# Requests to ScalarE that may pass one another, memsets and three products moved to VectorE, a DMA moved to GpSimd's queue, and another order on SyncE

## The chip, the cores and the metric

The kernel runs on one core of a Trainium2 chip. The core has five engines that work side by side, each through its own list of instructions in order: TensorE (PE, matrix products; PEld is its weight load), VectorE (DVE), ScalarE (ACT), GpSimd (POOL) and SyncE (SP), which here only issues DMAs. Semaphores order the lists against each other. The metric is the device time of one execution in microseconds; three executions of the kernel before took 570.37, 576.92 and 570.92 us, and their median, 570.92 us, is the time before.

## The reference

Two layers in a row. The first is a gated linear attention over 4 batches, 8 heads, 768 steps and 40 channels; the second a mixture of experts over the 3072 resulting rows of 320, each of which goes to the best two of eight experts by noisy gate values.

```python
for t in range(S):                       # per batch and head
    m_new = np.maximum(f_gate[:, :, t] + m, i_gate[:, :, t])
    f_stab = np.exp(f_gate[:, :, t] + m - m_new)
    i_stab = np.exp(i_gate[:, :, t] - m_new)
    m = m_new
    C = f_stab * C + i_stab * outer(vt, kt)
    n = f_stab * n + i_stab * kt
    y[:, :, t] = sigmoid(o_gate[:, :, t]) * (C @ qt) / maximum(abs(n @ qt), 1)

x = y.transpose(0, 2, 1, 3).reshape(3072, 320)
noisy = x @ w_gate + log1p(exp(x @ w_noise)) * noise
top2 = the best two columns of noisy;  w = exp(v - v.max()), divided by its sum + 1e-9
out[row] += w[k] * (relu(x[row] @ w1[e]) @ w2[e])      # for the two experts e of a row
```

All values are float32. The kernel keeps the matrix products of the experts near float32 precision by splitting each operand into a rounded high part and a low rest and adding three products.

## The kernel before

**Two stages.** The attention stage works in 24 units (`NU`), each of 64 steps of two groups of heads, so 128 rows of x. The expert stage takes the eight experts one after another: rows are gathered by token number, transposed, multiplied by w1 (L887), by w2 (L905 to L907), scaled, and added to the output by a scattered DMA (L931). All lists are written by hand in the order in which the program text runs; nothing reorders them later.

**A pass of the loop (L758).** Pass i works on several units at once, in this order of program text. The names are those of the prediction.

- At its head the DMAs: weights of choices that wait in the list `sent` (L762), the loads of unit i+3 (`load_unit`, L144 for q and k, L147 and L148 for v, k and the output gate), the copy of the rows of unit i-1 to DRAM (`keep_rows`, L377; POOL's queue issues it for units up to 11, SP's later), the moves of the gate values (`gate_move`, L212 and L214; POOL's queue up to pass 12, then SP's), pieces of w1 and w2 of the first expert (L117, L120, L724). Only four buffers exist for a unit's loads, so the v load of unit i+3 waits until unit i-1 is done with its buffer, and `keep_rows(i-1)` waits for the rows of i-1. SP takes these in order.
- `p_part(i+1)` (L337 on DVE): score products times decay weights, p(i+1).
- `c_part(i)` (L351 on PE, L354 on ACT): the state for the next unit. `o_part(i)` (L360 on PE): the output products, into PSUM bank o, of which there is one buffer. `e_part` (L298 on PE, L301 on ACT): decay exponents for unit i+2, one half here, one half later in the pass.
- `f_part(i)`, f(i) in the prediction (L365 to L373 on DVE): the division; then xr(i) (L374 on POOL): the product with the sigmoid of the output gate, 128 rows of x.
- logits of unit i-2 (`l_part`, L405 on PE), ranks that a group has asked for (`r_part`, L414 to L416), a burst that adds a group's token numbers to a table (`b_part`, L425, when no ranks are due), the transposes of rows i-1 (`t_part`, L385), and ACT's copies of all these (L389, L454, L457, L434).
- scores of unit i+2 (`s_part`, L319 and L323 on PE), the sigmoid of unit i+1 (`sig_part`, L306 to L308 on ACT), the decayed keys of unit i+2 (`k_part`, L331 on DVE).

**The routing (`g_part`, L470).** Four units make a group. When a group's logits are there, a generator puts its small operations into the lists bit by bit: `fill` (L629) lets it run at fixed places of a pass until a budget of estimated DVE time is used (1.8 us a pass), and a generator that yields "wait" gives up its turn. Its stages: softplus of the noise scale (exponent and logarithm on ACT), the best two by MAX8 and FIND_INDEX8 (L511, L514), d, the difference of the two (L517 on POOL), its exponent on ACT, the marks m and their running sums (L527, L535), ranks from PE (L559), places in the table (L575 to L589), weights (L549, L550), and the one-hot operands OA and OB of the burst (L596, L602). When four groups are in the table, `decode` (L438, on DVE) turns it into token numbers for the first four tiles of expert 0, and POOL issues their four gathers (L716) at the head of the last pass.

**ACT's requests.** The generator does not issue its ACT operations itself. It appends them to `acts`, and `act()` (L645), which stands at three places of a pass, issues all that are there. The generator waits until the list is empty, whoever filled it:

```python
acts.append((d, d, AF.Exp))          # L518, right behind d = P.tensor_sub(...)
...
while acts:                          # L537, ahead of the request for ranks
    yield "wait"
```

**The weights' way to DRAM.** A row of DRAM tile `rows` holds 320 values of x and then two weights. The generator computes the weights (L549, L550) as soon as d's exponent is there and appends the DMA to `sent`; SP issues it at the head of the next pass (L762), or in `tell` behind the loop.

**Constants.** `constants()` (L263) runs once, at pass 6: zeros in the unused half of w1's low part (64x1024), a row of zeros that later clears the output (128x320), the table (128x56) and the weights' tile (128x384), all by POOL, and a cast of token numbers by DVE (L265). Two more casts by DVE follow it (L793, L794).

## Time and profile before

| | us |
|---|---|
| median of three executions | 570.92 |
| the profiled execution | 572.61 |
| its span on the core | 570.5 |
| PE busy in the span | 545.3 |
| DVE busy | 352.4 |
| ACT busy | 254.9 |
| POOL busy | 244.0 |
| attention stage, until the first product of expert 0 | 151.7 |

The profiled execution's own time is 2.1 us above its span. How its rows are read: a row of a timeline starts with its start and its duration in us, then engine, source line, operation, output<-inputs by the program's names, shape and count; a bracket at its end tells how long the engine was idle before it and what ended that. A row of the windows view gives, for a stretch of time, each engine's busy time and its number of instructions, the clock granted to TensorE (1.00 is full) and the share of the DMA engines. A row of groups ends with busy time, mean ns of one, and the idle time before the group with its releasers. Busy time of PE is modelled from pipelined products, so a busy PE need not be at its peak.

### The profile page before, as it was taken

Reading aid. Unit: us, or ns where it says so; the run is one execution under the profiler, and the core shown is the slowest. Engines: PE = TensorE matmul, PEld = TensorE weight load, DVE = VectorE, ACT = ScalarE, POOL = GpSimd, SP = SyncE. Lnnn points to the kernel's source line nnn. Section 1 sums busy time; section 2 is a strip of 40 time slices with the busy share of each in tenths; the row PEclk is TensorE's granted clock in tenths of the full one; section 3 lists DMA queues with packets and bytes.
Section 4 is the critical chain, followed back from the end, with each engine's and each line's share of the span. In section 5 each row is a group of like instructions: output and inputs, shape, how many; then the busy total and the mean of one; then the engine's idle time right before and its main releaser. Section 6 shows DMA issues by size and latency. Waiting matters only on the chain.

```text
span 570.5 us, 13345 instructions
## 1 busy us (share of the span) xinstructions
PE 545.3 (96%) x5158; PEld 494.8 (87%) x5158; DVE 352.4 (62%) x937; ACT 254.9 (45%) x621; POOL 244.0 (43%) x336
## 2 busy tenths in 40 slices
PE   8799898999699999999999999999999999999995
PEld 3588787888479898998899899889989998998995
DVE  8889999998594386654563565466356545644511
ACT  6576778876241354522541442254145225414500
POOL 7446676533456546046224604532460453241043
PEclk9799899998699899999999999999999999999998
DMA  5887889795379365264326326432642543232023
GB/s 142 190 212 209 210 203 219 213 236 152 105 235 312 85 114 128 93 152 71 114 42 146 90 93 149 63 99 59 150 96 93 143 58 85 79 40 25 2 31 47
DMA packets 41060, 71.11 MB, mean 125 GB/s; under 512 B 8761, under 2 KB 30478, under 8 KB 40992
## 3 DMA queue, kind: packets, MB, share of 16 engines
q1 hardware_dynamic: 29632, 51.23, 31.8%
q0 software_dynamic: 11360, 18.98, 19.3%
q8 instruction: 42, 0.69, 0.5%
q14 instruction: 26, 0.21, 0.1%
HBM read 52.76 MB, written 17.73 MB: 124 GB/s over the span
## 4 chain that ended last, share of the span: by engine, by line
PE 80%; DVE 8%; DMA 5%; ACT 3%; issue 2%; POOL 1%; SPq 1%; POOLq 0%; DVEq 0%
PE s L887 22%; PE e L887 11%; PE st L907 5%; PE st L906 5%; PE st L905 5%; PE o L907 4%; PE o L906 4%; PE o L905 4%; PE s L746 3%; PE s L323 3%; DMA vk<-vk_in 2%; PE o L360 2%; PE e L298 2%; PE st L351 2%; PE xt L405 1%
## 5 line engine op out<-in xcount | busy, mean ns | idle before, releaser
L931 POOL DMA_INDIRECT y_out<-y,tok x56 | 87.1, 1556 | 220.5 <-DVE y L921 219.8
L887 PE MATMUL s<-xh,w1h 128*128 128x512 f32 (+1 forms) x255 | 78.0, 361 | 1.5 <-DVE xh L750 0.9
L893 DVE SCALAR_TENSOR_TENSOR hlo<-s,hh 128x512 fp32r<-128x512 f32 (+1 forms) x85 | 47.4, 558 | 41.2 <-ACT hh L892 36.7
L748 ACT ACTIVATE xh<-s 128x384 fp32r<-128x384 f32 (+1 forms) x56 | 25.4, 469 | 103.2 <-PE s L746 102.9
L716 POOL DMA_INDIRECT xg<-rows,tok x56 | 58.4, 1043 | 26.2 <-issue 16.8
L892 ACT ACTIVATE hh<-s 128x512 fp32r<-128x512 f32 (+1 forms) x85 | 41.7, 491 | 48.6 <-PE s L887 46.5
L887 PE MATMUL s<-xh,w1l 128*128 128x512 f32 (+1 forms) x255 | 63.1, 356 | 0.0
L905 PE MATMUL st<-w2h,hh 128*128 128x320 f32 x184 | 58.0, 315 | 0.0
L907 PE MATMUL st<-w2h,hlo 128*128 128x320 f32 x184 | 57.2, 311 | 0.0
L906 PE MATMUL st<-w2l,hh 128*128 128x320 f32 x184 | 56.8, 309 | 0.0
L887 PEld LDWEIGHTS s<-xh,w1h 128*128 128x128 f32 x255 | 46.2, 190 | 7.9 <-ACT xh L748 2.0
L905 PE MATMUL o<-w2h,hh 128*128 128x320 f32 x168 | 53.0, 315 | 0.0
L907 PE MATMUL o<-w2h,hlo 128*128 128x320 f32 x168 | 52.4, 312 | 0.0
L906 PE MATMUL o<-w2l,hh 128*128 128x320 f32 x168 | 51.9, 309 | 0.0
L887 PEld LDWEIGHTS s<-xh,w1l 128*128 128x128 f32 x255 | 45.1, 190 | 6.0
L887 PE MATMUL s<-xl,w1h 128*128 128x512 f32 (+1 forms) x170 | 46.6, 355 | 0.5 <-DVE xl L749 0.5
L374 POOL TENSOR_TENSOR xr<-tm,vk 128x320 f32<-128x320 f32 x24 | 22.2, 926 | 43.0 <-DVE tm L373 12.9
L887 PE MATMUL e<-xh,w1h 128*128 128x320 f32 (+1 forms) x129 | 39.7, 363 | 0.0
L749 DVE TENSOR_TENSOR xl<-s,xh 128x256 fp32r<-128x256 f32 (+1 forms) x56 | 22.6, 404 | 26.9 <-ACT xh L748 23.3
L323 PE MATMUL s<-qk 64*64 64x64 f32 x768 | 36.2, 233 | 0.7 <-issue 0.7
L921 DVE TENSOR_SCALAR y<-st,gw 128x320 f32<-128x320 f32 x23 | 12.7, 551 | 39.2 <-PE st L907 39.2
L893 DVE SCALAR_TENSOR_TENSOR hlo<-e,hh 128x256 fp32r<-128x256 f32 (+1 forms) x43 | 23.8, 554 | 18.8 <-ACT hh L892 17.9
(203 smaller groups left out, 1368.7 us busy)
## 6 DMA issues: line engine op xcount, KB each, us to landing
vk<-vk_in SPq DMA_DIRECT2D x48, 242.0 KB
raw<-w_in SPq DMA_DIRECT2D x7, 1280.0 KB
qk<-qk_in SPq DMA_DIRECT2D x48, 160.0 KB
raw<-w_in SPq DMA_DIRECT2D x7, 1024.0 KB
y_out<-zrow SPq DMA_DIRECT2D x15, 320.0 KB
raw<-w_in SPq DMA_DIRECT2D x18, 256.0 KB
rows<-xr POOLq DMA_DIRECT2D x12, 160.0 KB
rows<-xr SPq DMA_DIRECT2D x12, 160.0 KB
```

Of the source, the lines that this page charges most:

```text
L323: T.matmul(SQ[u][:, p][half[p], h, :], q[r, 1, h, :], q[r, 0, h, :], start=True, stop=True)
L374: P.tensor_mul(XR[u], tm.rearrange("p h d -> p (h d)"), SG[u % 4])
L716: P.indirect_dma_start(out=XG[0:rows_of(t), t], out_offset=None, in_=XD[0:n], in_offset=bass.IndirectOffsetOnAxis(ap=token(e, t), axis=0), ...
L748: A.activation(XH[:, :, c], ps[:, :, 0:n], AF.Copy)
L749: V.tensor_sub(XL[:, :, c], ps[:, 0:2, 0:n], XH[:, 0:2, c].bitcast(F32))
L887: T.matmul(ps[:, 0:n], l, r, start=i == 0, stop=i == len(ops) - 1)
L892: A.activation(HH[:, f, c], ps[:, 0:m], AF.Relu)
L893: V.scalar_tensor_tensor(HLO[:, f, c], ps[:, 0:m], 0.0, HH[:, f, c].bitcast(F32), op0=OP.max, op1=OP.subtract)
L905: T.matmul(ps, HH[:, j, c], W2H[:, j], start=j == 0, stop=False)
L906: T.matmul(ps, HH[:, j, c], W2L[:, j], start=False, stop=False)
L907: T.matmul(ps, HLO[:, j, c], W2H[:, j], start=False, stop=j == 7)
L931: st = P.indirect_dma_start(out=out, out_offset=bass.IndirectOffsetOnAxis(ap=token(e, t), axis=0), in_=y[0:n], in_offset=None, compute_op= ...
```

## The change

Five edits, all in the attention stage and in the routing.

1. `act()` keeps a count with each request, and `ask` makes one. A request with `late` 2 is issued at the third `act()` instead of the next; requests behind it are not held. Each generator waits for its own request alone. Only the exponent of d is asked for with `late` 2. The request for ranks now comes ahead of the wait for it.
2. The four memsets of `constants()` go to DVE, and the whole function, with the three casts, runs at pass 5.
3. The weights are computed at the end of the group's small operations, ahead of OA and OB, and POOL's queue issues their DMA there. `sent` stays empty.
4. At the head of a pass SP issues the q and k load, the gates' moves and the pieces of w1 and w2 first, and then the v load and the copy of rows, which wait for the unit before.
5. xr of units 21, 22 and 23 is computed by DVE instead of POOL.

```diff
+XP = 21
...
     def constants():
-        P.memset(W1L[0:64, 2].bitcast(F32), 0.0)
+        V.memset(W1L[0:64, 2].bitcast(F32), 0.0)
         V.tensor_copy(toki, cs[:, C_TOK:C_TOK + NU])
-        P.memset(zrow, 0.0)
-        P.memset(TBL, 0.0)
-        P.memset(WTS, 0.0)
+        V.memset(zrow, 0.0)
+        V.memset(TBL, 0.0)
+        V.memset(WTS, 0.0)
...
-        P.tensor_mul(XR[u], tm.rearrange("p h d -> p (h d)"), SG[u % 4])
+        (P if u < XP else V).tensor_mul(XR[u], tm.rearrange("p h d -> p (h d)"), SG[u % 4])
...
-        acts.append((ue, na, AF.Exp))
-        while acts:
+        a = ask(ue, na, AF.Exp)
+        while a[0] >= 0:
             yield "wait"
...
-        acts.append((d, d, AF.Exp))
+
+        a = ask(d, d, AF.Exp, 2)
...
         acc[g] = base[:, :, nb]
-        while acts:
+        rk = sm("rk", [128, NE * nb + 8])
+        asked = [m[:, :, 1:], base[:, :, 0:nb], base[:, :, nb], rk, False, unit[0] + (g < 3)]
+        want.append(asked)
+        while not asked[4] or a[0] >= 0:
             yield "wait"
         dd = sm("dd", [128, nb])
         P.tensor_scalar(dd, d, 1.0, 1e-9, op0=OP.add, op1=OP.add)
         e12 = OVM[:, u0:u0 + nb, 0:2]
         P.tensor_copy(e12, mi[:, :, 0:2])
-        yield
-        rk = sm("rk", [128, NE * nb + 8])
-        asked = [m[:, :, 1:], base[:, :, 0:nb], base[:, :, nb], rk, False, unit[0] + (g < 3)]
-        want.append(asked)
-        wt = WTS[:, u0:u0 + nb, 0:2]
-        yield "wait"
-        V.reciprocal(wt[:, :, 0], dd)
-        P.tensor_mul(wt[:, :, 1], d, wt[:, :, 0])
-        yield
-        sent.append((XD.rearrange("(u p) c -> p u c", p=128)[:, u0:u0 + nb, DM:RW], WTS[:, u0:u0 + nb]))
-        while not asked[4]:
-            yield "wait"
...
-        P.tensor_mul(OVM[:, u0:u0 + nb, 2:4], wt, ov)
         yield
         bi = sm("bi", [128, 2 * nb])
         V.scalar_tensor_tensor(bi, ai, -128.0, f(r), op0=OP.mult, op1=OP.add)
+        wt = WTS[:, u0:u0 + nb, 0:2]
+        yield
+        V.reciprocal(wt[:, :, 0], dd)
+        P.tensor_mul(wt[:, :, 1], d, wt[:, :, 0])
+        P.tensor_mul(OVM[:, u0:u0 + nb, 2:4], wt, ov)
+        P.dma_start(XD.rearrange("(u p) c -> p u c", p=128)[:, u0:u0 + nb, DM:RW], WTS[:, u0:u0 + nb])
...
     def act():
 
-        while acts:
-            A.activation(*acts.pop(0))
+        for a in list(acts):
+            if a[0] == 0:
+                A.activation(*a[1])
+                acts.remove(a)
+            a[0] -= 1
+
+    def ask(o, i, f, late=0):
+
+        a = [late, (o, i, f)]
+        acts.append(a)
+        return a
...
-        while sent:
-            SP.dma_start(*sent.pop())
         if 1 <= i and i + 3 < NU:
-            load_unit(i + 3)
-        if i:
-            keep_rows(i - 1)
+            load_unit(i + 3, "k")
...
             early_w2(2 * (i - W2AT), 2)
+
+        if 1 <= i and i + 3 < NU:
+            load_unit(i + 3, "v")
+        if i:
+            keep_rows(i - 1)
...
-        if i == 6:
+        if i == 5:
             constants()
```

More of the change, by code (lines that the diff above doesn't have):

```diff
@@ L488, in g_part @@
         ln = sm("ln", [128, nb, NE])
-        acts.append((ln, t1, AF.Ln))
+        a = ask(ln, t1, AF.Ln)
         co = sm("co", [128, nb, NE])
@@ L495, in g_part @@
         V.tensor_mul(co, co, na)
-        while acts:
+        while a[0] >= 0:
             yield "wait"
@@ L645, in act @@
     def act():
-        while acts:
-            A.activation(*acts.pop(0))
+        for a in list(acts):
[7 more added lines that the diff above has]
+        return a
     def warm(n):
```

## The prediction

> **What bounds the kernel now.** I read the page's head, slices and chain first, then busy time by stage, then the idle brackets of each engine's timeline in the attention stage.
>
> ```profile
> span 570.5 us, 13345 instructions
> ...
> PE 545.3 (96%) x5158; PEld 494.8 (87%) x5158; DVE 352.4 (62%) x937; ACT 254.9 (45%) x621; POOL 244.0 (43%) x336
> ...
> DVE  8889999998594386654563565466356545644511
> ```
>
> ```profile
> core 0: us, PE busy (x) PEld busy (x) DVE busy (x) ACT busy (x) POOL busy (x), PEclk, DMA share, GB/s
> ...
> 87.00:108.00 21.00, 20.31 (x456) 17.74 (x456) 20.12 (x64) 17.07 (x44) 10.75 (x20) 1.00 0.90 226
> ...
> 152.00:205.00 53.00, 51.20 (x291) 46.33 (x291) 30.27 (x106) 18.05 (x50) 28.41 (x42) 0.92 0.65 182
> ```
>
> The expert stage, from 152 us on, keeps PE busy (51.20 of 53.00) and the change leaves its matmuls alone. What can move is the attention stage before it, and there the averages mislead: DVE is at 62% over the span but at eight or nine tenths in the first ten slices. From 87 to 108 us PE and DVE are both full (20.31 and 20.12 of 21.00). Which of them bounds? PE has real holes there, and most end with ACT's exponent (the view of waits, 18 to 156 us: waiter, releaser, us, times, longest):
>
> ```profile
> PE e L298 <- ACT w L301: 5.5, 4, 2.4
> ...
> PEld s L319 <- DMA qk<-qk_in: 0.5, 2, 0.2
> ```
>
> DVE's timeline from 41 to 142 us carries an idle bracket on three rows alone:
>
> ```profile
> 67.15 0.69 DVE L559 TENSOR_TENSOR oh<-oh,rk 128x64 f32<-128x64 f32 x1 [0.77 <-ACT rk L457]
> ...
> 108.48 0.86 DVE L559 TENSOR_TENSOR oh<-oh,rk 128x64 f32<-128x64 f32 x1 [0.44 <-ACT rk L457]
> ...
> 141.44 0.27 DVE L486 TENSOR_SCALAR t<-ue 128x32 f32<-128x32 f32 x1 [1.67 <-ACT ue L648]
> ```
>
> So while PE stands still for ACT, DVE goes on working off its list, and PE catches up with it afterwards. Until about 140 us I take DVE as the bound: what shortens DVE's list or closes its three holes shortens the stage; a hole of PE that closes is worth what DVE lets through.
>
> **The change part by part.** Unit i is pass i of the loop; p(i), f(i) and xr(i) are its products, its division and its gated rows.
>
> *Constants' memsets to DVE, a unit earlier.* Six DVE rows of units 5, 6 and 10, three of POOL's, two DVE memsets of the start:
>
> ```profile
> 50.77 0.84 DVE L265 CAST toki<-cs 128x24 int32<-128x24 f32 x1
> 51.52 0.21 DVE L793 CAST tri<-cs 128x128 bf16<-128x128 f32 x1
> ...
> 54.13 2.80 DVE L486 TENSOR_SCALAR t<-ue 128x32 f32<-128x32 f32 x1
> ...
> 57.46 0.19 DVE L495 TENSOR_TENSOR co<-co,na 128x32 f32<-128x32 f32 x1
> ...
> 76.92 0.17 DVE L486 TENSOR_SCALAR t<-ue 128x32 f32<-128x32 f32 x1
> ...
> 77.62 0.48 DVE L495 TENSOR_TENSOR co<-co,na 128x32 f32<-128x32 f32 x1
> ```
>
> ```profile
> 50.27 1.31 POOL L374 TENSOR_TENSOR xr<-tm,vk 128x320 f32<-128x320 f32 x1 [2.77 <-ACT vk L307]
> ...
> 54.03 0.97 POOL L264 MEMSET w1l<- 64x1024 f32 x1
> ...
> 55.69 0.88 POOL L374 TENSOR_TENSOR xr<-tm,vk 128x320 f32<-128x320 f32 x1
> ```
>
> ```profile
> 1.42 0.91 DVE L162 MEMSET qk<- 32x1024 f32 x1 [0.27 <-issue]
> ...
> 3.62 0.27 DVE L170 MEMSET raw<- 64x256 f32 x1
> ```
>
> The same small DVE operation (L486) takes 0.17 us in the second group of units and 2.80 in the first, where POOL's memsets (the first at 54.03) and then xr(6), until 56.57, run beside it: DVE was held out. Without that train: 0.17 - 2.80 = -2.63. Late next is what xr(6) then meets, as in the other groups L495: 0.48 - 0.19 = +0.3. The cast of toki ran beside POOL's xr(5); a unit earlier it meets no such row, and I price it like the cast after it: 0.21 - 0.84 = -0.6 (bounds 0 and -0.6). The memsets cost DVE, by its two rows, (0.91 - 0.27) / 768 = 0.83 ns an element: 0.91 for w1l (1024), 0.32 for zrow (320), 0.38 for wts (384), 0.10 for the table (56), together +1.7. They stand ahead of p(6) and f(5) in DVE's list; nothing covers them. Sum in units 5 to 7: -2.63 + 0.3 - 0.6 + 1.7 = -1.2.
>
> Their side effect is on PE:
>
> ```profile
> 49.63 0.49 DVE L373 TENSOR_TENSOR tm<-o,dn 128x320 f32<-128x320 f32 x1
> ```
>
> ```profile
> 50.49 1.10 PE L360 MATMUL o<-vk,p 128*64 128x41 f32 x32
> ...
> 86.94 0.50 PE L298 MATMUL e<-re,le 98*128 98x512 f32 x1 [1.42 <-ACT w L301]
> ...
> 128.86 0.49 PE L298 MATMUL e<-re,le 98*128 98x512 f32 x1 [1.00 <-ACT w L301]
> ```
>
> ```profile
> 62.00:64.00 2.00, 2.00 (x50) 1.91 (x50) 1.90 (x6) 1.02 (x3) 1.60 (x4) 0.50 0.36 115
> ...
> 86.00:88.00 2.00, 1.06 (x25) 0.82 (x27) 1.75 (x8) 1.94 (x7) 1.98 (x6) 1.00 1.04 259
> ...
> 130.00:132.00 2.00, 1.99 (x40) 1.70 (x34) 1.93 (x8) 1.29 (x3) 1.60 (x6) 0.50 1.08 256
> ```
>
> PSUM bank o has one buffer, so the matmuls of o(6) wait for f(5), which ends at 50.12, 0.4 us ahead of them. With the memsets' 1.7 and the three casts' 0.6 in front of it, which stood behind it before, f(5) ends 2.3 us later and PE gets a hole of about 1.9 us, in place of the one in unit 7 that L486 made. That is DVE's own list again and no further cost, unless the clock follows. After a hole of 1.42 us the granted clock stayed at 1.00 (86 to 88); after one of 1.00 us it was 0.50 (130 to 132). A slow stretch of two to three microseconds costs PE half of itself, up to 1.5, part of which PE's lead takes up; I take nothing and keep +1.5 for the range. The Trainium skill, "TensorE: Matmul & The Clock Gate", section "What's actually happening", has the clock halve after an idle window of about 3.4 us. By that rule a hole of 1.9 us costs nothing and the sum stands; by the row at 128.86 it can cost the 1.5. The trace disagrees with the page here (0.50 after 1.00 us), so the row sets the bound.
>
> *ACT's requests.* Before, the exponent of d goes into ACT's list at the next chance, and ACT stands until POOL has made d:
>
> ```profile
> 83.92 0.21 ACT L648 ACTIVATE d<-d 128x4 f32<-128x4 f32 x1 [2.28 <-POOL d L517]
> ...
> 125.84 0.21 ACT L648 ACTIVATE d<-d 128x4 f32<-128x4 f32 x1 [1.85 <-POOL d L517]
> ```
>
> Behind it wait the gates, the state's copy and the exponent that PE needs: the holes at 86.94 and 128.86. Two places later d is long there and these holes go; under a full DVE that is worth nothing by itself. But PE comes earlier to what DVE does wait for: the idle at 67.15 (0.77, just after PE's stretch at 0.50) and at 108.48 (0.44) ends with a rank that PE makes. I take -0.5 and -0.4 (bounds 0 and -1.2 together). The rank is asked for in the same unit as before.
>
> *Last x by DVE (u 21 to 23).*
>
> ```profile
> L374 POOL TENSOR_TENSOR xr<-tm,vk 128x320 f32<-128x320 f32 x24 | 22.2, 926 | 43.0 <-DVE tm L373 12.9
> ...
> L730 DVE TENSOR_TENSOR w2l<-raw,w2h 128x320 fp32r<-128x320 f32 x56 | 27.1, 483 | 0.0
> ```
>
> Each costs DVE about 0.5 (L730's form) where POOL took 0.93. xr(21) lengthens DVE's list by 0.5 but no longer holds up the operation beside it (0.3 to 0.6 by L495 and toki): 0 (bounds -0.1 and +0.5). xr(22) falls into the idle before 141.44; xr(23) stands behind the decode, with slack.
>
> *The tail.*
>
> ```profile
> 143.05 1.16 POOL L716 DMA_INDIRECT xg<-rows,tok  x1 [1.39 <-DVE dn L365]
> ```
>
> ```profile
> 151.70 1.22 PE L887 MATMUL s<-xh,w1h 128*128 128x512 f32 x2 [0.58 <-ACT xh L748]
> ```
>
> Four gathers start when DVE has decoded the table, and the experts 151.70 - 143.05 = 8.65 us after the first, a chain that stays. The decode stands in DVE's list behind L486 and its 1.67 us of idle, which ends with ACT, which comes behind PE's burst, late by the hole at 128.86 and the slow clock. With PE on time that idle goes and xr(22) takes 0.5 of its place: -1.2 (bounds 0 and -1.7).
>
> *Weights by POOL's queue; SP's order.* The issues of POOL, the xr that comes behind the weights of the first group, its transpose on PE, and a run of DVE's beside it:
>
> ```profile
> L377 POOL DMA_DIRECT2D rows<-xr x12: 587/606/634, 25.8 to 85.4; - x12
> ```
>
> ```profile
> L716 POOL DMA_INDIRECT xg<-rows,tok x56 | 58.4, 1043 | 26.2 <-issue 16.8
> ```
>
> ```profile
> 72.54 0.89 POOL L374 TENSOR_TENSOR xr<-tm,vk 128x320 f32<-128x320 f32 x1
> ```
>
> ```profile
> 76.22 0.55 PE L385 MATMUL xt<-cs,xr 128*128 128x128 f32 x3
> ```
>
> ```profile
> 72.37 2.30 DVE L602 TENSOR_SCALAR ob<-cs,bi 128x128 fp32r<-128x128 f32 x6
> ```
>
> An issue by POOL's queue costs it 0.61 us for 128 rows, a gather of 128 1.04; the weights are 512 short rows, so 0.61 is the low bound and four gathers, 4.2, the high one; I take 0.61, the same kind of instruction. It stands behind the group's last product in units 8, 12, 16 and 20; behind it wait the split of W1, the row copies and the next xr. xr(9) ends at 73.43 and its transpose starts at 76.22, 2.8 us later; PE comes up to 0.9 earlier (the two idles), so about 2 us of slack cover the 0.61: 0 (bounds in the rivals). On SP the gates' moves (from unit 14), W1's and W2's pieces now go ahead of v and the row copies, up to five issues, and SP loses one. Loads hardly make anybody wait (qk: 0.5 in all, at PE's weight load): 0, with +0.5 for a late v.
>
> **Sum.** -1.2 (units 5 to 7) - 0.9 (two idles) + 0 (xr) - 1.2 (tail) = -3.3 us. The profiled execution took 572.61 us, 2.1 more than its span; it would take 569.3. The median shown is 570.92, 1.7 below that execution, so I predict 570.9 - 3.3 = 567.6.
>
> **Rivals.** (a) PE is the bound after all. Then its holes count in full: 5.5 for e, less the 0.7 of them at 20 us that nothing touches, and two slow stretches of 1.5: -7.8, to 563.1. For it: PE 20.31 of 21.00. Against: DVE's list has no idle across those holes. (b) Nothing comes out: the new hole in unit 6 halves PE's clock (+1.5) and the tail keeps its idle (+1.2), or POOL's operations, shifted, hold up other DVE rows by as much: -0.6, 570.3. For it: the 0.50 after a hole of 1.00. (c) Slower: the weights' issue goes by rows, 4.2 us on POOL, in units 8 and 12, where the split of W1 and the row copies also queue on POOL; past 2 us the next xr is late for its transpose, PE stops, and the clock halves: (4.2 - 2 + 1.5) x 2 = +7.4, less the gain +4.1, 575.0. Against: it is the instruction of the 0.61. (d) DVE's run of L602 holds up the issue for its 2.30 us, 2.9 in all: (2.9 - 2 + 1.5) x 2 = +4.8, less the gain +1.5, 572.4. Against: 587 to 634 ns over twelve issues beside a DVE that is full. The Trainium skill, "SBUF — State Buffer", section "SBUF: two separate sides", has this rule: a DMA's descriptors wait on POOL while DVE runs an operation on both its ports, and it advises the other queues. The trace so far does not agree (the spread of 47 ns).
>
> **How the numbers follow.** The forecast 0.60; (a) 0.07; (b) 0.25; (c) 0.04; (d) 0.04. The forecast's own bounds run from 565.2 (1.2, 1.7 and 0.1 in place of 0.9, 1.2 and 0, and a slow stretch of 1.5 less in the expert stage, whose clock is 0.92 from 152 to 205) to 570.3, where (b) begins; with (b), and an uncertainty of the median of some 0.5, the range is 565.0 to 571.0. A measurement of this kernel tells 2% (11.4 us) from no change; no case reaches it: faster 0.01, same 0.98, slower 0.01.
>
> **What would show it.** L486 at 0.2 in unit 6 and four memset rows of DVE, 1.7 together, in unit 5; a hole of PE before o(6); no ACT idle before d; no PE hole in units 12 and 20, with DVE still without idle brackets; the first gather some 3 us earlier, and 8.65 us from it to the experts. It is wrong if DVE shows new idle in units 8 to 20 (then PE, ACT or a load bounds), if the weights' issue on POOL is far from 0.61, or if POOL's xr meets longer DVE rows than before.

## The result, and the profile after

The changed kernel takes 577.28 us (median of 20 executions) against 571.41 for the kernel before (20 executions on the same chip): ratio 1.0124, 95% interval 1.0107 to 1.0142. The medians here and below are of all executions; the ratios leave out executions in a slower state, of which the kernel before had some and the changed kernel none, so they are not the quotients of the medians. The result is 9.7 us above the 567.6 that was predicted, and outside the range 565.0 to 571.0. It is slower by less than the 2% that the prediction counted as a change, but clearly so, where 0.6% faster was forecast.

The head of the profile of the changed kernel, whose profiled execution took 579.39 us:

```profile
span 577.6 us, 13330 instructions
...
PE 548.4 (95%) x5158; PEld 497.7 (86%) x5158; DVE 360.3 (62%) x944; ACT 253.8 (44%) x621; POOL 242.5 (42%) x335
```

DVE is busy 7.9 us longer (352.4 before). The memsets and the three x add 1.72 and 1.48 of it; the rest is not new work. Four marks split the span's 7.1 us: the first gather starts at 147.20 (143.05 before), +4.2; from there the first product of expert 0 comes after 10.43 (8.65), +1.8; the expert stage up to the last row of the group `s<-xh,w1h` is 0.3 shorter; from that row to the end it takes 32.6 (31.1), +1.5. The windows of the changed kernel up to the first expert, and then one row of the kernel before (columns: stretch, its length, busy time and count of PE, PEld, DVE, ACT, POOL, granted clock, DMA share, GB/s):

```profile
87.00:108.00 21.00, 20.09 (x423) 17.56 (x421) 20.17 (x58) 16.00 (x42) 11.17 (x20) 0.92 0.76 209
108.00:130.00 22.00, 20.28 (x439) 17.78 (x441) 21.07 (x62) 16.09 (x43) 10.50 (x17) 1.00 0.75 203
130.00:147.20 17.20, 15.05 (x334) 13.56 (x328) 16.20 (x54) 11.29 (x31) 5.58 (x13) 0.97 0.51 142
147.20:157.63 10.43, 6.82 (x28) 4.82 (x28) 5.89 (x32) 2.80 (x8) 4.37 (x5) 0.50 0.85 291
```

```profile
143.05:151.70 8.65, 4.10 (x18) 2.56 (x18) 4.81 (x28) 2.41 (x8) 5.68 (x8) 0.70 0.48 147
```

DVE stays full up to the first gather (20.17 of 21.00, 21.07 of 22.00), so it bounds this stage as the prediction had it. In the last stretch the DMA engines are at 0.85 in the changed kernel and at 0.48 before.

**Held rows.** Where the time of DVE went is in its groups between 20 and 150 us (columns: line, engine, operation, output<-inputs, count, busy us, mean ns, idle before). First the kernel before, then the changed one:

```profile
L602 DVE TENSOR_SCALAR ob<-cs,bi 128x128 fp32r<-128x128 f32 x32 | 11.3, 425 | 0.0
...
L506 DVE TENSOR_TENSOR nl<-ln,lg 128x32 f32<-128x32 f32 x5 | 1.0, 192 | 0.2
L503 DVE TENSOR_TENSOR ln<-ln,nzt 128x32 f32<-128x32 f32 x5 | 1.0, 192 | 0.2
```

```profile
L601 DVE TENSOR_SCALAR ob<-cs,bi 128x128 fp32r<-128x128 f32 x32 | 13.4, 505 | 0.0
L508 DVE TENSOR_TENSOR nl<-ln,lg 128x32 f32<-128x32 f32 x5 | 3.0, 602 | 0.2
...
L505 DVE TENSOR_TENSOR ln<-ln,nzt 128x32 f32<-128x32 f32 x5 | 2.0, 405 | 0.2
```

The same operations on the same shapes: nl takes 602 ns in the mean and not 192, ln 405 and not 192. These three groups alone are 5.1 us longer. The timelines say what held them. In the kernel before, POOL's subtraction for w1's low part (L137, six times) began within 0.6 us of DVE's p. The six are called here by the units in which they run in the changed kernel, 9, 10, 13, 14, 17 and 18. The first of them, with its p:

```profile
70.31 1.28 POOL L137 TENSOR_TENSOR w1l<-raw,w1h 128x512 fp32r<-128x512 f32 x1
```

```profile
70.20 1.22 DVE L337 TENSOR_TENSOR p<-s,w 128x1024 f32<-128x1024 f32 x1
```

In the changed kernel, POOL's rows and then DVE's:

```profile
71.45 0.87 POOL L588 DMA_DIRECT2D rows<-wts  x1
72.35 1.29 POOL L139 TENSOR_TENSOR w1l<-raw,w1h 128x512 fp32r<-128x512 f32 x1
...
74.47 0.88 POOL L376 TENSOR_TENSOR xr<-tm,vk 128x320 f32<-128x320 f32 x1
...
81.14 1.27 POOL L139 TENSOR_TENSOR w1l<-raw,w1h 128x512 fp32r<-128x512 f32 x1 [1.24 <-ACT w1h L138]
```

```profile
70.80 1.22 DVE L339 TENSOR_TENSOR p<-s,w 128x1024 f32<-128x1024 f32 x1
...
72.97 3.35 DVE L601 TENSOR_SCALAR ob<-cs,bi 128x128 fp32r<-128x128 f32 x6
...
81.17 1.29 DVE L508 TENSOR_TENSOR nl<-ln,lg 128x32 f32<-128x32 f32 x1
```

p is over at 72.02; POOL issues the weights from 71.45 to 72.32, and only then subtracts, beside the run of one-hot operands, which takes 3.35 us where it took 2.30. In unit 10 the subtraction, which waits for ACT's w1h, catches nl: 1.29 us for an operation of 0.19. p, which takes one of its inputs from PSUM, is not held (1.22 beside the subtraction and 1.22 without it). To put a number on it, each DVE row that overlaps one of the six subtractions is taken less the shortest row of its line and shape in the whole trace: the sum of these excesses is 0.30 us before and 6.55 after. Over all DVE rows between 20 and 150 us it is 15.7 before and 20.7 after ("held time" below).

The trace also shows that the loss arises where these rows are. From the end of tm of unit 7 to that of unit 20 the changed kernel takes 72.73 us and the kernel before 67.52, so 5.2 more; in this stretch DVE's held time is 5.7 longer and its idle time 0.4 shorter.

The Trainium skill, "SBUF — State Buffer", section "Who interferes with whom", has the rule: a DVE instruction with two SBUF inputs, or in a two-port mode, which a tensor_scalar can enter, contends with a GpSimd instruction that reads SBUF, and the later one is blocked for the whole of the other; with at most one SBUF input and outside those modes it does not. The trace agrees in both halves: nl and ln (two SBUF inputs) take 0.95 to 1.10 us longer beside a subtraction, ob (a tensor_scalar) 0.71 to 1.49 (the longest of them runs on into xr), and p does not wait.

**Gathers.** POOL's first gather, SP's copies of zeros to the output in the changed kernel, and those copies before:

```profile
147.20 1.12 POOL L724 DMA_INDIRECT xg<-rows,tok  x1 [1.98 <-DVE km L447]
```

```profile
149.18 14.55 SPq L277 DMA_DIRECT2D y_out<-zrow  x16
```

```profile
149.50 0.96 SPq L275 DMA_DIRECT2D y_out<-zrow  x2
```

The copies of zeros, 320 KB each, stand on SP's queue behind the row copy of unit 23. Before, xr(23) stood on POOL behind the four gathers, so the copies began 6.4 us after the first gather, and after two of them SP waited for the weights of the last group. Now DVE makes xr(23) at 148.27, the copies begin 2.0 us after the first gather, nothing stops them, and they meet the gathers: ten copies are issued ahead of the first product of expert 0, where it was two.

**The end.** The last row of POOL in the kernel before and in the changed one:

```profile
564.57 1.56 POOL L931 DMA_INDIRECT y_out<-y,tok  x1 [1.85 <-DVE y L921]
```

```profile
570.16 1.56 POOL L940 DMA_INDIRECT y_out<-y,tok  x1 [1.85 <-DVE y L930]
```

From its start to the end of the span pass 5.9 us before and 7.4 after. In the trace's records of POOL's sequencer two closing steps are longer: the update of its DMA queue's semaphores (1.24 us, 0.91 before) and the drain behind it (4.28, 3.45 before).

### The profile page after: what moved, and what is told of

It reads as the page before. It is cut to its first block, busy times and chain, and to the rows that moved or that the text cites. A ratio compares the mean times of both kernels' runs of the same rounds, so it can differ in the third digit from the quotient of the medians.

```text
span 577.6 us, 13330 instructions
## 1 busy us (share of the span) xinstructions
PE 548.4 (95%) x5158; PEld 497.7 (86%) x5158; DVE 360.3 (62%) x944; ACT 253.8 (44%) x621; POOL 242.5 (42%) x335
## 3 DMA queue, kind: packets, MB, share of 16 engines
q0 software_dynamic: 11552, 19.18, 19.3%
## 4 chain that ended last, share of the span: by engine, by line
PE 71%; DVE 14%; issue 4%; ACT 3%; DMA 3%; POOL 2%; SPq 1%; POOLq 0%; DVEq 0%
PE s L896 22%; PE e L896 10%; PE st L916 5%; PE st L915 5%; PE st L914 5%; PE o L916 4%; PE o L915 4%; PE o L914 4%; PE s L754 3%; DVE ob L601 3%; DVE p L339 3%; DVE kd L333 1%; PE o L362 1%; PE o L922 1%; PE o L923 1%
## 5 line engine op out<-in xcount | busy, mean ns | idle before, releaser
L376 POOL TENSOR_TENSOR xr<-tm,vk 128x320 f32<-128x320 f32 x21 | 21.0, 1000 | 49.8 <-DVE tm L375 21.9
L757 DVE TENSOR_TENSOR xl<-s,xh 128x256 fp32r<-128x256 f32 (+1 forms) x56 | 22.6, 404 | 27.4 <-ACT xh L756 27.3
L303 ACT ACTIVATE w<-e 128x512 f32<-128x512 f32 x46 | 27.6, 600 | 20.3 <-PE e L300 20.1
```

What stands on the lines that cost most here:

```text
L303: A.activation(W[u][:, p].rearrange("p h t -> p (h t)"), ps, AF.Exp)
L757: V.tensor_sub(XL[:, :, c], ps[:, 0:2, 0:n], XH[:, 0:2, c].bitcast(F32))
```

## The experiments

Names with u start from the changed kernel, names with b from the kernel before. The first four were one group; T1 is DVE's list with POOL's subtraction holding its rows, T2 late loads of v by SP's new order, T3 the hole of PE in unit 6 and the slow clock behind it ("theory 1" to "theory 3" in their expectations). The later ones speak of theory A, which is T1, theory B, the copies of zeros that meet the gathers, and theory C, POOL's closing steps that grow longer by the weights' issues.

| kernel | median us | ratio to before, 95% | held time | gather to expert | last product to end |
|---|---|---|---|---|---|
| before | 571.41 | 1 | 15.7 | 8.65 | 31.1 |
| after | 577.28 | 1.0124 (1.0107 to 1.0142) | 20.7 | 10.43 | 32.6 |
| u_const | 578.81 | 1.0143 (1.0067 to 1.0219) | 19.4 | 11.33 | 32.3 |
| u_sp | 578.98 | 1.0154 (1.0077 to 1.0230) | 19.8 | 11.01 | 32.3 |
| u_route | 575.02 | 1.0034 (0.9983 to 1.0086) | 15.5 | 9.59 | 31.1 |
| u_nosplit | 574.78 | 1.0070 (1.0031 to 1.0110) | 14.7 | 10.92 | 32.6 |
| u_tied | 576.78 | 1.0113 (1.0073 to 1.0152) | 16.3 | 11.37 | 32.3 |
| u_xp | 576.61 | 1.0103 (1.0059 to 1.0146) | 19.3 | 8.96 | 32.3 |
| u_spw | 574.98 | 1.0070 (1.0031 to 1.0109) | 16.2 | 9.31 | 31.2 |
| u_best | 573.02 | 1.0019 (0.9978 to 1.0059) | 16.3 | 8.51 | 31.1 |
| b_xp | 569.98 | 0.9994 (0.9968 to 1.0019) | 16.0 | 9.48 | 31.0 |
| b_poolw | 576.92 | 1.0068 (1.0028 to 1.0109) | 17.0 | 8.59 | 32.6 |
| u_late0 | 582.26 | 1.0187 (1.0125 to 1.0249) | 17.7 | 10.61 | 32.6 |
| u_best2 | 571.76 | 1.0025 (1.0000 to 1.0051) | 17.8 | 8.62 | 31.2 |
| b_hit | 575.25 | 1.0011 (0.9964 to 1.0059) | 16.7 | 8.94 | 31.1 |
| u_wlate | 574.71 | 1.0066 (1.0031 to 1.0101) | 18.0 | 9.03 | 32.3 |
| u_best4 | 570.74 | 0.9976 (0.9946 to 1.0005) | 14.1 | 8.48 | 31.1 |
| b_hit2 | 578.77 | 1.0137 (1.0082 to 1.0192) | 22.6 | 8.96 | 31.2 |

The last three columns are us of the profiled execution; "last product" is the last row of the group `s<-xh,w1h`. Held time differs by up to 1.3 among kernels in which the subtractions stand as in the kernel before (b_xp 16.0, b_hit 16.7, b_w1 17.0), so a smaller difference in it says little. The first gather's own time is not in the table, because single executions scatter there: b_xp, the same as the kernel before up to pass 21, had it at 139.87, the kernel before at 143.05. The profiled executions of u_xp and b_poolw took 587.05 and 583.36 us, far above their medians; of them only the order of events and the numbers in the table are read.

Two columns sort all kernels without exception. With the last x on POOL the first expert comes 8.48 to 9.03 us after the first gather, with it on DVE after 9.31 to 11.37: after 9.31 to 9.59 where SP stops behind two copies of zeros to wait for the weights, and after 10.43 or more where ten copies run. The end takes 32.3 to 32.6 us where POOL issues all six of the weights' DMAs, and 31.0 to 31.2 elsewhere.

**u_const**: the memsets on POOL at pass 6 again, as before.

```diff
-        V.memset(W1L[0:64, 2].bitcast(F32), 0.0)
+        P.memset(W1L[0:64, 2].bitcast(F32), 0.0)
...
-        if i == 5:
+        if i == 6:
             constants()
```

> The changed kernel with the memsets by POOL at pass 6 as before. Theory 1: DVE loses 1.7 us of memsets and gets back the hold-up of 2.6 at L486 less what xr does there now (1.0), so 577 within 1.5; the split stays at its bad place unless the phase moves. Theory 3: no hole of PE in unit 6, 572 or less. Theory 2: 577.

1.0143: nothing is won. Edit 2 is not the cause, nor is T3 with it, since this kernel has no hole ahead of o(6).

**u_sp**: the v load and the row copy at the head of the pass again, as before.

```diff
-            load_unit(i + 3, "k")
+            load_unit(i + 3)
+        if i:
+            keep_rows(i - 1)
```

> The changed kernel with SP's and POOL's order at the head of a pass as before. The changed kernel was 1.2 us ahead by the division of unit 4, where nothing but this order differs. Theory 1: that 1.2 is lost, 577 to 579 us. Theory 2: v comes in time again, 572 or less. Theory 3: 577.

1.0154: T2 falls.

**u_route**: the kernel before with edits 2, 4 and 5, so the changed kernel with the routing and ACT's requests of before.

> The changed kernel with the routing as before: ACT's requests in order, weights early and by SP's queue. Memsets by DVE, SP's order and the last x by DVE stay. Theory 1: the subtraction for w1 goes back beside p, 571 to 573.5 us. Theory 2 or 3: 577. If the requests' order matters for PE, ACT stands again before d in units 7, 11 and 19, and DVE's list shows no new idle for it.

1.0034, and the subtractions are beside p again (excess 1.37 us, one of six held). Most of the loss lies in edits 1 and 3.

**u_nosplit**: POOL writes zeros in place of the subtraction for the first expert, so this kernel leaves the low part of w1 out of that product.

```diff
-                lo.tensor_sub(W1L[n, k, s], RAW1[n, k, s], W1H[n, k, s].bitcast(F32))
+                if lo is P:
+                    P.memset(W1L[n, k, s].bitcast(F32), 0.0)
+                else:
+                    lo.tensor_sub(W1L[n, k, s], RAW1[n, k, s], W1H[n, k, s].bitcast(F32))
```

> The changed kernel, but POOL writes zeros to the low part of the first expert's w1 in the attention stage instead of subtracting (this low part of the product is left out). The operation then reads nothing and lasts some 0.5 us instead of 1.28. Theory 1 (DVE's list is the bound, and the 7 us come from DVE operations held out while POOL subtracts for w1 beside them, where the subtraction used to fall beside the products p): the six held-up rows of units 9, 10, 13, 14, 17, 18 fall by some 1 us each, 571 to 573 us. Theory 2 (loads of v, issued later on SP, are late): as the changed kernel, 577. Theory 3 (the hole of PE in unit 6 and the slow clock behind it): 577.

1.0070: 3 us less, with the held time at 14.7. T1 has the sign; but a kernel with less work can't tell place from work, and 4 us stay. In its profiled execution the stretch from tm of unit 7 to tm of unit 20 is 67.87, close to the 67.52 of the kernel before.

**u_tied**: the six subtractions with the same work, issued just ahead of the next p, behind a DVE memset of one column.

```diff
                 A.activation(W1H[:, k, s], RAW1[:, k, s], AF.Copy)
+                if lo is P:
+                    yield
+                    V.memset(W1L[n, k, f:f + 1].bitcast(F32), 0.0)
                 lo.tensor_sub(W1L[n, k, s], RAW1[n, k, s], W1H[n, k, s].bitcast(F32))
...
+        if W1AT <= i - 1 < W1AT + 12 and (i - 1) % 2 == 0:
+            next(pre1)
         if i + 1 < NU:
             p_part(i + 1)
```

> The changed kernel, with POOL's subtraction for the first expert's w1 put beside p by a dependence: its issue moves from the end of a pass to just ahead of p of the next one, and a DVE memset of one column of the same tile (about 0.1 us, six times) stands between, so that POOL can't begin before DVE has come to p. The work of POOL and ACT stays. Theory A (DVE's list bounds the attention stage, and the change moved this subtraction from beside p, where DVE reads PSUM and isn't held, to beside L601, L508 and L505, which it holds about 1 us each): the L508 and L505 rows go back to 0.2 us and L601's run to 2.3, the first gather comes 3 to 7 us earlier than the 147.2 of the changed kernel, and the median lies 3 to 6 us under its 577.3, at 571 to 574. Rival (a kernel without the subtraction is faster only because POOL has less work): the first gather stays within 1 us of 147.2 and the median at 576 to 578. In both, the gathers' 10.4 us to the first expert's matmul and the 32.6 us from the last matmul of w1's first half to the end stay.

A miss: 576.78. The memset is a lower bound only. In units 10, 14 and 18 the subtraction came beside p (excess 0.05 each), but in 9, 13 and 17 POOL was still busy with the weights and the row copy and began it at 73.21, beside the one-hot run (0.90 to 1.21 each; 3.34 over all six). The gathers met the zeros for longer, too (11.37).

**u_xp**: the changed kernel with `XP = 24`.

> The changed kernel with the last three xr on POOL again (XP = 24). Theory B (x of unit 23 by DVE comes free early, so that its row copy and, behind it on SP's queue, the copies of zeros to the output, 320 KB each, start 2 us after the first gather, and not 6.4 us after it, behind the gathers; the gathers then land after 4.2 to 4.8 us, and not after 3.0): the zeros start 6 us or more after the first gather, the gathers land after 3.0 us, the first expert comes 8.6 to 8.9 us after the first gather and not 10.4, and the median is 1.5 to 2 us lower, 575.5. Rival (the gathers are late for another reason: the weights' issue ahead of them on the same queue, or the slow TensorE clock): 10.4 stays, and the median is 577.

The zeros start 6.4 us after the first gather, and the first expert comes after 8.96 and not 10.43, near the 8.6 to 8.9 of theory B. The median, 576.61, is 0.7 lower where 1.5 to 2 were expected; the intervals of 1.0103 and 1.0124 overlap.

**u_spw**: the weights' issue on SP again, at the head of the next pass.

```diff
-        P.dma_start(XD.rearrange("(u p) c -> p u c", p=128)[:, u0:u0 + nb, DM:RW], WTS[:, u0:u0 + nb])
+        sent.append((XD.rearrange("(u p) c -> p u c", p=128)[:, u0:u0 + nb, DM:RW], WTS[:, u0:u0 + nb]))
...
+        while sent:
+            SP.dma_start(*sent.pop())
```

> The changed kernel with the weights' issue on SP again (at the head of the next pass). Theory C (the issues by POOL's queue make POOL's closing steps longer: its last drain 4.28 us and not 3.2 to 3.4, the step before it 1.25 and not 0.92): the stretch from the last matmul of w1's first half to the end is 31.1 us and not 32.6. By theory A POOL's subtraction begins 0.87 us earlier in the units 9, 13 and 17, ends before L601's run, and the first gather is 1 to 3 us earlier. SP waits again for the weights of the last group behind two copies of zeros, so the gathers take 9.6 us to the first expert and not 10.4. Together 3 to 5 us less: 572 to 574. Rival (the closing is longer for another reason, and the 0.87 is covered): 32.6 stays and the median is 576 to 578.

The end is at 31.2 (theory C holds), the gathers at 9.31, the subtractions' excess at 1.43. But 574.98 misses the 572 to 574, and SP's queue shows why (then the window 68 to 72 us):

```profile
62.53 0.55 SPq L150 DMA_DIRECT2D vk<-vk_in  x1
69.64 0.43 SPq L770 DMA_DIRECT2D rows<-wts  x1
70.13 0.80 SPq L146 DMA_DIRECT2D qk<-qk_in  x2
```

```profile
68.00:72.00 4.00, 4.00 (x85) 3.47 (x79) 3.90 (x11) 3.71 (x10) 3.75 (x8) 1.00 0.25 44
```

SP runs two passes ahead of the engines and stands 7 us for weights that are now made late; the DMA engines fall to 0.25 of their time, the loads behind come all together, and PE later has two holes of 2.5 us ahead of its scores.

**u_best**: u_tied, u_xp and u_spw in one.

> The changed kernel with all three: subtraction beside p, weights' issue on SP, last x by POOL. If theories A, B and C hold side by side: first gather at 139.5 to 142, 8.7 us to the first expert, 31.1 us at the end, so 3 us less than the kernel before: median 566.5 to 569, ratio to the kernel before 0.993 to 0.998. If only A holds: 571 to 574. If none: 577.

1.0019, 573.02: the loss is gone within the interval, though not by the 3 us under the kernel before that were expected; SP stands here as in u_spw.

**b_xp**: edit 5 alone, on the kernel before.

> The kernel before with one part of the change alone: xr of the units 21 to 23 by DVE. Theory B (x of unit 23 comes free before the gathers, so its row copy and the first two copies of zeros run beside them): the zeros start about 2 us after the first gather and not 6.4, the first expert comes 9.4 to 9.8 us after the first gather and not 8.65 (two copies only, since SP then waits for the weights of the last group), and with up to 0.5 us of DVE's list the median is 1 to 1.5 us over the kernel before, ratio 1.000 to 1.004. Rival (the copies don't matter to the gathers): 8.65 stays, ratio 0.998 to 1.001.

9.48 and not 8.65 from the first gather to the expert, as theory B has it, but no measurable cost: 0.9994, just under the range.

**b_poolw**: the weights' issue by POOL alone, on the kernel before.

```diff
-        sent.append((XD.rearrange("(u p) c -> p u c", p=128)[:, u0:u0 + nb, DM:RW], WTS[:, u0:u0 + nb]))
+        P.dma_start(XD.rearrange("(u p) c -> p u c", p=128)[:, u0:u0 + nb, DM:RW], WTS[:, u0:u0 + nb])
```

> The kernel before with one part alone: the weights' issue by POOL's queue, at the place where before they were put on the list for SP. Theory C: POOL's closing steps are longer, so the stretch from the last matmul of w1's first half to the end is 32.6 us and not 31.1; the issue takes POOL 0.8 to 0.9 us ahead of the xr of units 8, 12, 16 and 20, which has slack. xr of unit 23 stays on POOL behind the gathers, so the copies of zeros come behind them and the first expert 8.6 to 9 us after the first gather. Median 1.5 to 3 us over the kernel before, ratio 1.002 to 1.006. Rival (the closing has to do with something else in the changed routing): 31.1, ratio 0.998 to 1.002.

1.0068, a little over the range, with 32.6 at the end: theory C by itself, in the old routing. That is 1.5 of some 3.9 us; the subtractions' excess is 1.36 here (one of six held), and the rest is not accounted for.

**u_late0**: d's exponent at the next place of ACT's list, `ask(d, d, AF.Exp)` without the 2.

> The changed kernel with the exponent of d in ACT's list at the next place and not two places later. ACT stands again about 2 us before d, and PE again before e. Theory A (DVE bounds; what counts is beside which of DVE's operations POOL's subtraction falls, and it waits for ACT's w1h in the units 10, 14 and 18): the stand of ACT costs nothing by itself, and the first gather moves by as much as the held-up time of DVE's rows does, within 2 us of 147.2 in either direction; median 575 to 578. Rival (PE's holes count, the late request was a gain): first gather 149 or later, median 579 or more.

582.26: here theory A fails. PE has its holes ahead of e again (1.42, 0.67 and 1.88 us), and the time is that of the rival, though the first gather, at 146.51, is not. The late request seems to be the part of the change that pays: 1.0187 against 1.0124, so some 3.6 us, with intervals that overlap at their edges. The trace does not show it well: the profiled execution (580.51, in the lower half of the six) has a span only 1.2 longer than that of the changed kernel, and the stretch from tm of unit 7 to tm of unit 20 is 2.1 shorter.

**u_best2**: last x by POOL, weights on SP two passes after they are made.

```diff
+        while sent and (sent[0][0] <= i - 2 or done[0] >= E0U[0]):
+            SP.dma_start(*sent.pop(0)[1:])
```

> The changed kernel with the last x by POOL and the weights' issue on SP, two passes after they are made (in u_spw and u_best SP stood at the head of pass 9 from 62 to 71 us for them, DMA fell to 0.25 in 68 to 72 us, and the loads behind it landed after 9 us, with PE stalls of 2.3 to 2.5 us for qk); no tie of the subtraction. Theories A, B, C together: no such stand of SP; POOL's subtraction ends before L601's run; first gather at 141.5 to 144, 8.6 us to the first expert, 31.1 us at the end: median 568 to 571.5, ratio 0.995 to 1.002, so the loss of the change is gone. Rival (something else of the new routing costs the attention stage): first gather at 146 or later, median 573 or more.

571.76, 1.0025: 0.3 us over the range, with each term where theories A, B and C put it (142.32, 8.62, 31.2). The excess is 0.41 in units 9, 13 and 17 (3.43 in the changed kernel), and still 1.07 and 0.96 in units 14 and 18.

**b_hit**: in the kernel before, three subtractions were to be put beside L602.

```diff
         f_part(i, (lambda: fill(0.15, False)) if i + 2 < NU else (lambda: None))
+        if W1AT <= i < W1AT + 12 and i % 4 == W1AT % 4:
+            j = (i - W1AT) // 2
+            V.memset(W1L[64 * (j % 3 == 2):128, j % 3, 512 * (j // 3):512 * (j // 3) + 1].bitcast(F32), 0.0)
```

> The kernel before, with the same work, but POOL's subtraction for w1 in the units 9, 13 and 17 may begin only when the division of the pass is done (a DVE memset of one column, 0.06 us, three times, stands ahead of it), so it falls beside L602's run as in the changed kernel and not beside p. Theory A: DVE's rows beside the six subtractions lose 3 to 4 us instead of 0.30, the next xr is pushed into the same run, and the end of the attention stage is 2.5 to 4.5 us later: median 573.5 to 575.5, ratio 1.004 to 1.008. Rival (where the subtraction falls doesn't matter to the time): ratio 0.998 to 1.002.

Inconclusive: the memset lay a unit too early, the subtractions stayed beside p (excess 0.35), and 1.0011 says only that the memsets cost nothing.

**u_wlate**: as u_best2, but `P.dma_start` at that place.

> As u_best2, but the weights' issue goes to POOL's queue, two passes after the weights are made, so it doesn't stand ahead of the subtraction. If the place is what costs (theory A), only the closing steps are left: 32.6 us and not 31.1 at the end, median 1.5 us over u_best2's 571.8 (572.5 to 574), first gather at 141.5 to 144. If POOL's queue as such costs the attention stage: first gather at 145 or later, median 575.5 or more, like u_xp's 576.6.

574.71 and a first gather at 144.34, each just past the first case and short of the second. Held time is 18.0 (17.8 in u_best2), the end 32.3: over u_best2 it costs 2.3 us, of which 1.1 at the end. Away from the subtraction, the queue as such no longer holds the stage; the first case is the nearer.

**u_best4**: as u_best2, with the subtractions of units 10, 14 and 18 put beside p as in u_tied.

```diff
+                if lo is P and (f // 512 + k) % 2:
+                    yield
+                    V.memset(W1L[n, k, f:f + 1].bitcast(F32), 0.0)
...
+        if W1AT <= i - 3 < W1AT + 12 and (i - 3) % 4 == 0:
+            next(pre1)
```

> As u_best2, with the three subtractions that still collide there (units 10, 14 and 18: excess 0.03, 1.07 and 0.96 us on L505 and L508) put beside p by a one-column DVE memset. Theory A: the excess falls from 2.47 to about 0.4 us, the first gather comes 1.5 to 2.5 us earlier than 142.3, and the median is 569 to 570.5, ratio 0.996 to 1.001. Rival (these rows don't bound the time): no change, 571 to 572.5, ratio 1.001 to 1.005.

The excess is 0.28 and the ratio 0.9976, against 1.0025 for u_best2 and 1.0124 for the changed kernel. The stretch from tm of unit 7 to tm of unit 20 is 67.60, as in the kernel before (67.52), against 72.73 in the changed one. The first gather (144.37) did not come earlier in the profiled execution, which was 3.1 us behind the kernel before at tm of unit 3 already (granted clock 0.51 from 20 to 41 us, 0.76 before). Its DVE groups are those of the kernel before:

```profile
L604 DVE TENSOR_SCALAR ob<-cs,bi 128x128 fp32r<-128x128 f32 x32 | 11.8, 442 | 0.0
...
L511 DVE TENSOR_TENSOR nl<-ln,lg 128x32 f32<-128x32 f32 x5 | 1.0, 202 | 0.2
...
L508 DVE TENSOR_TENSOR ln<-ln,nzt 128x32 f32<-128x32 f32 x5 | 1.0, 192 | 0.2
```

It is the fastest of these kernels; that it beats the kernel before is not shown (0.9946 to 1.0005).

**b_hit2**: what b_hit was to do; the subtraction of units 9, 13 and 17 is issued in `f_part`, behind tm of that unit.

```diff
+                if lo is P and (f // 512 + k) % 2 == 0:
+                    yield
+                    V.memset(W1L[n, k, f:f + 1].bitcast(F32), 0.0)
                 lo.tensor_sub(W1L[n, k, s], RAW1[n, k, s], W1H[n, k, s].bitcast(F32))
...
         V.tensor_mul(tm, ps[:, :, 0:D], dn[:, :, None].to_broadcast([128, H, D]))
+        if W1AT <= u - 1 < W1AT + 12 and (u - 1 - W1AT) % 4 == 0:
+            next(pre1)
```

> The kernel before, with the same work, but POOL's subtraction for w1 in the units 9, 13 and 17 can begin only when the division's last product tm of that unit is done (a DVE memset of one column, 0.06 us, three times), so it falls beside L602's run, as in the changed kernel, and not beside p. Theory A: DVE's rows beside the six subtractions lose 3 to 4 us instead of 0.3, xr behind it is pushed into the same run, and the end of the attention stage is 2.5 to 4.5 us later: ratio 1.004 to 1.008. Rival (where the subtraction falls doesn't matter to the time): ratio 0.998 to 1.002.

1.0137: the kernel before, with three subtractions moved behind memsets of one column and the rest of its work as it was, becomes as slow as the changed one. POOL's rows, DVE's rows and DVE's groups:

```profile
71.60 1.27 POOL L140 TENSOR_TENSOR w1l<-raw,w1h 128x512 fp32r<-128x512 f32 x1 [1.38 <-ACT vk L309]
72.83 0.86 POOL L379 TENSOR_TENSOR xr<-tm,vk 128x320 f32<-128x320 f32 x1
```

```profile
71.38 0.06 DVE L139 MEMSET w1l<- 128x1 f32 x1
71.61 3.05 DVE L607 TENSOR_SCALAR ob<-cs,bi 128x128 fp32r<-128x128 f32 x5
```

```profile
L607 DVE TENSOR_SCALAR ob<-cs,bi 128x128 fp32r<-128x128 f32 x32 | 14.4, 521 | 0.0
...
L508 DVE TENSOR_TENSOR ln<-ln,nzt 128x32 f32<-128x32 f32 x4 | 1.8, 452 | 0.1
L511 DVE TENSOR_TENSOR nl<-ln,lg 128x32 f32<-128x32 f32 x4 | 1.7, 430 | 0.1
```

The cost is 7.8 us where 2.5 to 4.5 were expected: xr behind the subtraction is pushed into the same run, and two of the other three subtractions, which were not touched, now meet ln and nl (excess 5.14 in all, held time 22.6). The held rows are not all of it: between tm of unit 7 and tm of unit 20 this execution is 9.8 longer than the kernel before, of which 4.7 is held time and 4.5 idle time of DVE, most of it (4.4) behind a slow stretch of PE (granted clock 0.66 from 115 to 130 us) that follows a hole of 1.48. Whether the moved subtractions cause that stretch is open.

**b_w1**: the kernel before with one of the six issues of the weights on POOL's queue.

> The kernel before with the weights of the first group alone issued by POOL's queue, those of the other five by SP. Theory C in two forms, told apart by the stretch from the last matmul of w1's first half to the end. If the longer closing goes with the number of issues: 31.1 + 1.5 / 6, at most 31.5. If one issue is enough (another kind of transfer on the queue): 32.6. In neither does the median tell, since 1.5 us is within the spread of single runs.

31.2 at the end (571.4 us, one execution): one issue adds at most 0.1 of the 1.5, less than the 0.25 of an even share, so it is not the mere presence of such a transfer. How the closing grows from one issue to six, and why, was not tried.

## Why the prediction was wrong

Held time, the stretch from gather to expert and the end add up. For the changed kernel they give (20.7 - 15.7) + (10.43 - 8.65) + (32.6 - 31.1) = 8.3 us, measured 0.0124 x 571 = 7.1; for b_hit2 7.2 and 7.8, for u_best2 2.1 and 1.4, for u_best4 -1.8 and -1.4, for u_wlate 3.9 and 3.8. All kernels of the table agree within 1.5 us but three: u_tied (4.5 and 6.5), u_spw (1.2 and 4.0, SP's stand) and u_late0 (5.4 and 10.7, ACT's stand). A ladder of single steps takes the loss apart: from the changed kernel to u_xp 1.2 us (last x, within the intervals), to u_best2 4.5 (weights off POOL's queue and away from the subtraction), to u_best4 2.8 (the other three subtractions beside p; these two intervals overlap).

- **The step that failed** is the weights' issue: "about 2 us of slack cover the 0.61: 0". The issue took 0.84 us in the mean, not far off, and the xr behind it had its slack: PE never stood for its transpose. But the split of W1, which the working names as queued behind it, was looked at only for being late for somebody. It isn't late; it is moved out from beside p into the rows of DVE that it holds. That is 3.0 us in units 9, 13 and 17 (3.43 in the changed kernel against 0.41 in u_best2). The held rows of units 10, 14 and 18, 3.12 us against 0.13 before, were in no term of the sum either. How many of these three collide changes from kernel to kernel (three in the changed one, two in u_best2, one in u_route, u_spw and u_late0), and what decides it was not isolated. The longer closing of POOL's queue, 1.5 us, was in no term.

```profile
L588 POOL DMA_DIRECT2D rows<-wts x4 | 3.4, 843 | 0.0
```

- **Rival (b)** had the mechanism, "POOL's operations, shifted, hold up other DVE rows by as much", and the last sentence of the prediction named something near it, POOL's xr meeting longer DVE rows; it was the subtraction for w1. Its size was set at the size of the gain (2.7), and the held time grew by 5.0. Rivals (c) and (d) had the instruction and a slower kernel (575.0 and 572.4, measured 577.28), but by a late transpose and by a blocked issue; neither happened.
- **DVE as the bound** was right: no idle bracket on DVE after the one at 68.04 and up to 145 us. That is why held time came through in full between units 7 and 20 (5.7 of held time, 5.2 of the stretch).
- **The last x** cost DVE 0.49 each, as priced. "A chain that stays" was wrong: 8.65 became 10.43, because an xr that is free early lets SP send zeros beside the gathers. b_xp (9.48) and u_xp (8.96) show it, and so does every other kernel of the table. Alone it costs under the measurement (0.9994); with the weights off SP's queue nothing stops the zeros after the second.
- **Units 5 to 7.** The four memsets took 1.72 us (1.7 predicted), and the hole ahead of o(6) is there. L488 fell to 1.17 and not 0.17, since it now meets xr(6) itself (54.55 to 55.42):

```profile
51.16 1.09 PE L362 MATMUL o<-vk,p 104*64 104x41 f32 x16 [2.25 <-DVE tm L375]
```

```profile
54.61 1.17 DVE L488 TENSOR_SCALAR t<-ue 128x32 f32<-128x32 f32 x1 [0.27 <-ACT ue L648]
```

  The rows sum to 1.7 - 1.6 - 0.7 (toki, 0.84 before and 0.10 now) = -0.6 in place of -1.2, and the slow clock behind the hole, which was kept for the range alone, came (0.79 in the mean from 41 to 65 us, 0.93 before). u_const (1.0143) shows that the end doesn't depend on it.
- **ACT's requests**: ACT no longer stands for d in the four groups of the loop, and the idle at 108.48 is gone, the one of 0.8 at 68.04 stayed. The sum had 0.9 and 1.2 (with the tail) for it; u_late0 suggests 3.6, so there probably was a gain, buried under the held rows. Why u_late0 loses 5.3 us more than its three terms give is not settled; DVE has idle there that the changed kernel does not have (0.32, 0.37, 0.17 and 1.15 us at 110, 133, 142 and 145 us), which is 2.0 of it.
- **SP's order** was worth nothing, as predicted (u_sp).

## What to carry to other kernels

When an edit delays an engine's list, ask not only who waits for the delayed operation but beside what it will now run: if two engines hold each other on some operands and not on others, the phase between their lists is worth as much as the work. Look for such pairs by comparing the mean with the shortest row of one shape, and pin the costly one to a harmless partner by a dependence rather than by luck; the dependence only says when it may begin, so nothing else may stand ahead of it (u_tied). An operation that finishes earlier lets its followers start: name the transfers queued behind it and what they will meet.

## What the runs showed of the hardware

- A subtraction of 1.28 us on POOL holds a DVE operation of 0.19 us for up to 1.1 us, and in b_hit2 three subtractions moved beside the run of one-hot operands, with all that they shift, go with 7.8 us.
- POOL's closing steps are longer with more DMAs issued by its queue: six issues of the weights add 1.1 to 1.5 us at the end of the span, one adds 0.1 at most.
- The granted clock does not follow the length of one hole. In the kernel before, PE's hole of 1.42 us ahead of 86.94 left it at 1.00; in u_route the same hole did this:

```profile
86.34 0.80 PE L298 MATMUL e<-re,le 98*128 98x512 f32 x1 [1.42 <-ACT w L301]
```

```profile
87.00:97.00 10.00, 9.98 (x145) 9.01 (x145) 8.05 (x20) 5.77 (x13) 5.59 (x11) 0.50 0.60 163
```

  Ten microseconds at half speed follow, and DVE, which is busy 8.05 of them, has room there. That may be why first gathers of single executions scatter by several us; it was not tested.
